# A third set of seven first-layer products in each group of a linear-attention and feed-forward kernel, with all of a group's work in one written order

## The chip, the core and the metric

The kernel runs on one core of a Trainium2 chip. A core has a matrix engine (TensorE, PE in the profile, with its weight loads as PEld), a vector engine (DVE), a scalar engine (ACT), a general engine (POOL) and SyncE (SP), which here issues transfers. Each engine runs its own instructions in program order and waits for others through semaphores. Matrix products go to PSUM, which has eight banks; everything else lies in SBUF. The metric is the time of one execution on the device in microseconds (us).

## What is computed

Retention (linear attention with a decay per head) over q, k and v, and behind it a feed-forward layer on the 4608 resulting tokens:

```python
B, H, S, D_ = q.shape                                  # 8, 8, 576, 64
scores = (1 / np.sqrt(D_)) * np.matmul(q, k.transpose(0, 1, 3, 2))
gamma = 1.0 - 2.0 ** (-5.0 - np.arange(H, dtype=np.float32))
rel = pos[:, None] - pos[None, :]
Dmat = np.where(rel >= 0, gamma[:, None, None] ** rel[None, :, :], 0.0)
attn = np.matmul(scores * Dmat[None, :, :, :], v)
x = attn.transpose(0, 2, 1, 3).reshape(B * S, H * D_)  # 4608 x 512
h = x @ w_in                                           # 512 x 2048
out = np.maximum(0.01 * h, h) @ w_out                  # 2048 x 512
```

## The kernel before

**Units and groups.** The tokens are cut into 36 units of 128 tokens (two chunks of 64; nine chunks make one sequence) and 9 groups of 512 tokens (four units). Group g is put through the feed-forward layer while the units of group g+1 go through retention.

**A unit u** passes these steps. `load` (L121) fetches k, q and v in f32, into a pool of six buffers per kind (`ld_pool`, L70). `cast_k` on ACT, `cast_q` and `cast_v` on POOL (L172 to L181) turn them to f16, with the decay. `transpose_dma` (L183) transposes q and k by a transfer that SP issues. `scores` (L211) makes 64 small products on TensorE's quarters, into the PSUM tile sc (two banks, one buffer): the scores, and the new part of the state. `masks` (L237) applies the causal mask, on DVE; with `aside` an ACT copy is followed by a POOL product. `state` (L257) adds to the running state on DVE, and `state_cast` (L284) makes its f16 copy on POOL. `outputs` (L297) of unit u-1 stands on TensorE right behind the scores of unit u: a first half that needs the masked scores, a second half that needs the f16 states of u-2 and u-1. It fills the PSUM tile ot (two banks, one buffer). `own` (ACT, L370) and `add` (DVE, L376) bring it to xT, the f16 input of the feed-forward layer. `burst` (L791) is these steps from the scores on; `ahead` (L808) is the casts and the transposition of unit u+2; `step` (L823) is both, with the load of unit u+4 between them.

**The first layer** has 16 blocks of 128 features. A plain block (`h_block`, L406) is four products of 128x512 columns into one PSUM bank, and a leaky ReLU on ACT. Four blocks at once (two from each half of the features) can be made by seven half-size products instead of eight, Strassen's scheme in Winograd's form: `h_seven` (L460). It uses sums of w_in (`sum_w_in`, L435, made once) and sums of x (`sum_x`, L447, four POOL operations per group), seven products p1, p1', p6, p5, p7, p5', p7' of four matmuls of 128x256 each, an ACT copy, five DVE additions and four activations. Two sets, at f = 0 and f = 4, make eight of a group's blocks. The other eight (2, 10, 3, 11, 6, 7, 14, 15) are plain. The products take turns in four PSUM banks (`acc_pool`, L80): a new product waits until the bank's contents of four turns ago are read.

**The second layer** is made by the same scheme over 16 blocks (`seven`, L574): seven products P1 to P7' of 16 matmuls of 128x256, with eight sums of the activations per group on DVE (`mix`, L560), some of which overwrite the activations, and sums of w_out made once (`mix_weights`, L545). Each half of a group's result is stored by one transfer of 512 KB on SP (`store`, L516). In the last group the second half is stored in four parts of 128 KB as they come.

**Order of the work.** `manual_schedule` leaves the order to the program text: each engine runs its instructions as they are written. For groups 2 to 8 it comes from nested calls (L949 on): `h_seven` takes plain blocks as fill and a burst in its middle, with some results of a set "owed" to the next one; the mixes and the second layer follow, with steps 7 and 8 in hooks between its products. Group 0 runs plain throughout, in halves as its units arrive; group 1 has a plain first layer, and its second layer is the first use of `seven`; steps 9 to 12 are called in between (`early`, L917, the table `at`, L922, and the hooks at L940). In the opening phase all loads up to unit 10 and the weights are requested on POOL's queue in a fixed order (L673 to L690), and matmuls on zeros (`keep_warm`, L660) fill waits.

```python
def burst(u, out=True, split=False):
    if u < NU:
        scores(u)
    if out:
        outputs(u - 1)
    ...
def early(u, n):
    burst(u)
    ahead(n, (lambda: sum_x(u // 4 - 1)) if u % 4 == 0 else None)
    load(n + 3)
```

## Time and profile before

| | |
|---|---|
| three runs | 283.15, 283.71, 283.88 us (median 283.71) |
| profiled execution | 283.58 us, span of its instructions 281.8 us |
| TensorE matmul busy | 274.0 us (97%), 4231 instructions |
| weight loads | 205.5 us (73%) |
| DVE | 211.7 us (75%) |
| ACT | 153.6 us (55%) |
| POOL | 155.8 us (55%) |
| DMA | 50.04 MB moved, mean 178 GB/s |
| mean granted TensorE clock | 0.997 |

The span runs from the first to the last instruction. Busy time is a union of intervals; matmuls overlap in their pipeline, so the price of a kind of matmul is best read from the distance between starts in the timeline, not from its own duration (a matmul of 128x256 lasts 0.273 us but four of them start 0.44 us after the four before). The same holds for DVE: an addition of 128x512 lasts 0.69 us, and an independent one starts 0.60 us later. In a line of the timeline the columns are start, duration, engine, source line, operation, output and inputs with shape, count, and in brackets the idle time just before it with what ended it.

### The profile page before, as it was taken

The numbers are of one execution on the slowest core, as the hardware profiler recorded it, in microseconds if no ns is written. First come the engines' busy times: TensorE is split into PE (matmuls) and PEld (weight loads), VectorE is DVE, ScalarE is ACT, GpSimd is POOL, SyncE is SP. The second block draws the span as 40 slices with busy tenths as digits, with TensorE's granted clock in tenths as the row PEclk, the third lists the DMA queues.
The fourth block names the chain that finished last, engine by engine and source line by source line (L and its number), as shares of the span: only waits on it lengthen the run. The fifth ranks groups of instructions, "written<-read, shape, count | busy, mean of one in ns | idle before, by whom it ended". The sixth has DMA issues, their size and how long they took to land.

```text
span 281.8 us, 9828 instructions
## 1 busy us (share of the span) xinstructions
PE 274.0 (97%) x4231; PEld 205.5 (73%) x4231; DVE 211.7 (75%) x360; ACT 153.6 (55%) x284; POOL 155.8 (55%) x173
## 2 busy tenths in 40 slices
PE   7899999999999999999999999999999999999994
PEld 3468888745886788678867886788678867886683
DVE  2884688998876887689777986898689677865772
ACT  3776777633337742774277427742774277416610
POOL 8968946735449507960796069607951693051000
PEclk9999999999999999999999999999999999999998
DMA  7999999998999987898689966986797151012004
GB/s 204 309 237 255 280 203 327 211 185 178 230 224 225 270 174 122 230 188 192 149 204 208 215 133 211 223 186 147 198 252 159 40 187 42 2 74 77 0 3 149
DMA packets 123100, 50.04 MB, mean 178 GB/s; under 512 B 112048, under 2 KB 116784, under 8 KB 123056
## 3 DMA queue, kind: packets, MB, share of 16 engines
q1 hardware_dynamic: 116032, 37.23, 59.7%
q0 software_dynamic: 6736, 12.06, 17.7%
q8 instruction: 33, 0.54, 0.8%
q10 hardware_dynamic: 288, 0.11, 0.1%
q14 instruction: 11, 0.09, 0.1%
HBM read 36.81 MB, written 9.44 MB: 164 GB/s over the span
## 4 chain that ended last, share of the span: by engine, by line
PE 87%; DMA 5%; POOL 4%; DVE 3%; issue 1%; ACT 0%; DVEq 0%; POOLq 0%
PE acc L591 35%; PE acc L390 24%; PE acc L471 15%; PE acc L528 5%; POOL t L134 3%; PE sc L221 3%; DMA w_in<-in_moe_w_in_dram 3%; DMA t<-in_v_dram 2%; PE ot L305 2%; PE sc L230 1%; PE ot L316 1%; POOL w_in L152 1%; DVE s L248 0%; DVE xT L377 0%; DVE s L272 0%
## 5 line engine op out<-in xcount | busy, mean ns | idle before, releaser
L390 PE MATMUL acc<-xT,w_in 128*128 128x256 f16 (+2 forms) x496 | 88.6, 318 | 0.1
L591 PEld LDWEIGHTS <-gt 128*128 128x128 f16 x640 | 61.3, 98 | 8.5 <-ACT gt L404 0.8
L404 ACT ACTIVATE gt<-acc 128x512 f16<-128x512 f32 x102 | 58.5, 597 | 13.6 <-PE acc L390 13.1
L390 PEld LDWEIGHTS <-w_in 128*128 128x128 f16 x496 | 45.4, 98 | 18.0 <-issue 0.2
L591 PE MATMUL acc<-w_out,gt 128*128 128x256 f16 x384 | 46.3, 273 | 0.2 <-ACT gt L404 0.2
L372 ACT COPY own<-ot 128x512 f32<-128x512 f32 x33 | 19.4, 587 | 40.3 <-PE ot L316 34.8
L287 POOL CAST st<-s 128x512 f16<-128x512 f32 x21 | 12.9, 612 | 48.3 <-DVE s L272 30.6
L177 POOL TENSOR_TENSOR qk<-t,cs 128x512 f16<-128x512 f32 x28 | 30.5, 1091 | 0.3 <-ACT gt L404 0.2
L591 PE MATMUL acc<-w_mix,gt 128*128 128x256 f16 x256 | 30.6, 273 | 0.0
L181 POOL TENSOR_TENSOR v<-t,cs 128x512 f16<-128x512 f32 x28 | 30.4, 1084 | 0.0
L591 PE MATMUL acc<-w_mix,mix 128*128 128x256 f16 x256 | 29.3, 273 | 0.0
L404 ACT ACTIVATE gt<-h 128x512 f16<-128x512 f32 x42 | 25.7, 629 | 6.0 <-DVE h L482 5.5
L471 PEld LDWEIGHTS <-w_sum 128*128 128x128 f16 x224 | 21.9, 98 | 8.6 <-issue 0.2
L591 PEld LDWEIGHTS <-mix 128*128 128x128 f16 x256 | 25.0, 98 | 3.0
L377 DVE TENSOR_TENSOR xT<-ot,own 128x512 f16<-128x512 f32 x33 | 22.5, 683 | 3.7 <-ACT own L372 3.7
L482 DVE TENSOR_TENSOR h<-acc,u 128x512 f32<-128x512 f32 x28 | 19.2, 686 | 6.0 <-PE acc L471 6.0
L174 ACT CAST qk<-t 128x512 f16<-128x512 f32 x36 | 22.5, 624 | 1.2 <-DMA t<-in_k_dram 1.2
L471 PE MATMUL acc<-x_sum,w_sum 128*128 128x256 f16 x168 | 22.9, 273 | 0.0
L241 POOL TENSOR_TENSOR s<-s,idle 128x512 f16<-128x512 f16 x12 | 13.9, 1160 | 15.8 <-ACT s L240 15.8
L482 DVE TENSOR_TENSOR u<-acc,k 128x512 f32<-128x512 f32 x14 | 9.7, 690 | 17.0 <-PE acc L471 17.0
L471 PEld LDWEIGHTS <-w_in 128*128 128x128 f16 x168 | 16.3, 97 | 6.8 <-DVE h L482 0.5
L489 ACT COPY k<-acc 128x512 f32<-128x512 f32 x14 | 8.2, 586 | 22.2 <-issue 17.0
(77 smaller groups left out, 436.1 us busy)
## 6 DMA issues: line engine op xcount, KB each, us to landing
out_dram<-osb SPq DMA_DIRECT2D x17, 512.0 KB, 4.6
t<-in_k_dram SPq DMA_DIRECT2D x24, 256.0 KB, 4.2
t<-in_q_dram SPq DMA_DIRECT2D x23, 256.0 KB, 4.5
t<-in_v_dram SPq DMA_DIRECT2D x22, 256.0 KB, 4.7
t<-in_v_dram POOLq DMA_DIRECT2D x10, 256.0 KB, 5.4
t<-in_q_dram POOLq DMA_DIRECT2D x9, 256.0 KB, 5.5
t<-in_k_dram POOLq DMA_DIRECT2D x8, 256.0 KB, 5.8
w_in<-in_moe_w_in_dram POOLq DMA_DIRECT2D x8, 256.0 KB, 6.9
```

The source lines that it names most:

```text
L174: nc.scalar.copy(out=qk16[u][:, 1], in_=t32[u, 1])
L177: eng.tensor_tensor(out=qk16[u][:, 0], in0=t32[u, 0], in1=decay(u, 0), op=MUL)
L181: eng.tensor_tensor(out=v16[u], in0=t32[u, 2], in1=decay(u, 1), op=MUL)
L241: nc.gpsimd.tensor_tensor(out=s16s[u], in0=s16s[u], in1=mask16.unsqueeze(1).unsqueeze(1).to_broadcast([P, 2, NP, CH]), op=MUL,)
L372: nc.scalar.copy(out=owns[u], in_=ot_tiles[u][:, :, 0:NP].rearrange("q j c t -> q c j t"))
L377: nc.vector.tensor_tensor(out=x_of(u).rearrange("q (c g) t -> q c g t", g=2), in0=ot_tiles[u][:, :, NP : 2 * NP].rearrange("q g (c j) t -> ...
L390: nc.tensor.matmul(out=hps[:, n, :], lhsT=w_in16[:, c, f * P : (f + 1) * P], rhs=xT[g][:, c, ts], start=(c == 0), stop=(c == NP - 1),)
L404: nc.scalar.activation(out=out, in_=in_, func=mybir.ActivationFunctionType.Lrelu)
L471: nc.tensor.matmul(out=r[name][:, n, :], lhsT=lhs[:, c, n * P : (n + 1) * P], rhs=rhs[:, c, :], start=fresh and n == 0 and c == 0, stop=c ...
L482: nc.vector.tensor_tensor(out=r[name], in0=r[a], in1=r[b], op=ADD)
L528: nc.tensor.matmul(out=ys[tb], lhsT=g_t[0][:, f, tb * P : (tb + 1) * P], rhs=w_out16[:, f, :], start=(f == 0), stop=(f == NF - 1),)
L591: nc.tensor.matmul(out=r[name][tb][:, 0, :] if apart else r[name][0][:, tb, :], lhsT=lhs[:, f, tb * P : (tb + 1) * P], rhs=rhs[:, f, :], s ...
```

## The change

- A third set of seven products at f = 2 replaces the plain blocks 2, 10, 3 and 11. Blocks 6, 7, 14 and 15 stay plain. The sums of w_in get a third tile. The two later sets of these sums are made on POOL instead of DVE, at point 13 of the table `at` and after burst 11.
- The nested calls are replaced by tables of named operations (`set_ops`, `block_ops`, `second_ops`, `step_ops`) and one string, GROUP, that lists all operations of a group in order. The last group has its own string, LAST, and some of its products go to the banks of sc and ot, which no burst uses then (`LAST_HOMES`).
- Partial sums in SBUF are updated in place, in two k, two v and one h buffer. The load pool has five buffers instead of six. A load of unit u+4 is issued behind the transposition of unit u+2.
- In the opening phase v of unit 4 is requested ahead of the third quarter of w_in, two more warming matmuls are added, and the load of unit 13 moves from point 1 to point 4 of the table. In group 1 burst 12 moves from behind P7 to ahead of it.

In the names of the strings, p1A is product p1 of set A (f = 0; B is f = 2, C is f = 4), k, u, v, h4, h5, h4' are its copy and additions, g00 to g11 its activations; blk15 and l15 a plain block and its activation; sc5 the scores of step 5 with the outputs of the unit before; s0, s1a, s1, stc the state and its cast; mc and msk the mask; kc, qc, vc the casts of the unit two ahead; m00 to m31 the mixes; x0 to x3 the sums of x; P1 to P7', K, U, V and o00 to o10 the second layer.

```diff
-    ld_pool = ctx.enter_context(tc.tile_pool(name="ld", bufs=6))
+    ld_pool = ctx.enter_context(tc.tile_pool(name="ld", bufs=5))
...
-    w_sum = const_pool.tile([P, 2, 4, NP // 2, 2 * P], F16, name="w_sum")
+    w_sum = const_pool.tile([P, 3, 4, NP // 2, 2 * P], F16, name="w_sum")
...
-    def masks(u, aside=False):
-        s16s[u] = b_pool.tile([P, 2, NP, CH], F16, name="s16")
-        if aside:
+    def masks_aside(u, part):
+        if part == 0:
+            s16s[u] = b_pool.tile([P, 2, NP, CH], F16, name="s16")
             nc.scalar.copy(out=s16s[u], in_=sc_tiles[u][:, :, 0])
+        else:
             nc.gpsimd.tensor_tensor(
                 out=s16s[u],
                 in0=s16s[u],
                 in1=mask16.unsqueeze(1).unsqueeze(1).to_broadcast([P, 2, NP, CH]),
                 op=MUL,
             )
-            return
+
+    def masks(u):
+        s16s[u] = b_pool.tile([P, 2, NP, CH], F16, name="s16")
...
-    def state(u, j):
+    def state(u, j, parts=(0, 1)):
...
+        if scaled and 0 in parts:
+            nc.vector.tensor_tensor(out=st, in0=st, in1=carry[0], op=ADD)
+        if 1 not in parts:
+            return
...
-    def sum_w_in(f, n):
-        t = w_sum[:, f // 4]
+    def sum_w_in(f, n, eng):
+        t = w_sum[:, f // 2]
...
+    def set_ops(g, f, s, homes):
...
+        ops = {
+            "p1": lambda: product("p1", ws(0, 0), xs(0, 0), True),
+            "k": keep,
+            "p1'": lambda: product("p1", ws(0, 1), xs(1, 0), False),
+            "g00": lambda: give(0, 0, "p1"),
+            "p6": lambda: product("p6", w(1), t(1), True),
+            "u": lambda: into(r["k"], r["p6"], r["k"]),
+            "p5": lambda: product("p5", w(0), t(0), True),
+            "v": lambda: fresh_sum("v", "v", "p5", "k"),
+            "p7": lambda: product("p7", w(2), t(2), True),
+            "h4": lambda: into(r["v"], r["p7"], r["v"]),
+            "p5'": lambda: product("p5", w(3), xs(1, 1), False),
+            "h5": lambda: fresh_sum("h", "h", "p5", "k"),
+            "g11": lambda: give(1, 1, "v"),
+            "p7'": lambda: product("p7", ws(1, 1), t(3), False),
+            "h4'": lambda: into(r["k"], r["p7"], r["k"]),
+            "g01": lambda: give(0, 1, "h"),
+            "g10": lambda: give(1, 0, "k"),
+        }
+        return {n + s: op for n, op in ops.items()}
...
-    def seven(g, last=False):
+    def second_ops(g, homes, last=False):
...
+    def step_ops(g, n):
+        u, w = 4 * g + n, 4 * g + n + 2
+        cast = []
+
+        def mm():
+            if u < NU:
+                scores(u)
+            outputs(u - 1)
+
+        def turn_when_cast(what, *a):
+            what(w, *a)
+            cast.append(0)
+            if len(cast) == 2:
+                transpose_dma(w)
+                if u > 13 and u + 4 < NU:
+                    load(u + 4)
+
+        ops = {
+            "sc": mm,
+            "own": lambda: own(u - 1),
+            "add": lambda: add(u - 1),
+        }
         if u < NU:
-            load(u)
-
-    def step(u, split=False):
-        rest = burst(u, True, split)
-        if u > 13:
-            fetch(u + 4)
-        if u % 4 == 0:
-            sum_x(u // 4 - 1, (0, 1))
-            ahead(u + 2, lambda: sum_x(u // 4 - 1, (2, 3)))
-        else:
-            ahead(u + 2)
-        return rest
+            ops["s0"] = lambda: state(u, 0)
+            ops["s1a"] = lambda: state(u, 1, (0,))
+            ops["s1"] = lambda: state(u, 1, (1,))
+            ops["stc"] = lambda: state_cast(u, pool_copy)
+            if n < 7:
+                ops["mc"] = lambda: masks_aside(u, 0)
+                ops["msk"] = lambda: masks_aside(u, 1)
+            else:
+                ops["msk"] = lambda: masks(u)
+        if w < NU:
+            ops["kc"] = lambda: turn_when_cast(cast_k)
+            ops["qc"] = lambda: turn_when_cast(cast_q, nc.gpsimd)
+            ops["vc"] = lambda: cast_v(w, nc.gpsimd)
+        return {name + str(n): op for name, op in ops.items()}
+
+    SETS = {"A": 0, "B": 2, "C": 4}
+    BLOCKS = (6, 7, 14, 15)
+    GROUP = """
+        p1A kA sc5 p6A qc5 s05 kc5 s1a5 p1'A mc5 p5A uA s15 blk15 own5 vA vc5 g00A add5 p7A
+        msk5 stc5 l15 p1B h4A p5'A h5A kB sc6 kc6 p7'A p1'B p6B mc6 own6 s06 h4'A g00B blk7
+        msk6 s1a6 qc6 p5B uB p1C s16 vB g01A l7 p6C add6 g10A p7B kC h4B g11A p5'B stc6 p1'C
+        g00C sc7 p7'B h5B uC s07 blk14 own7 msk7 p5C blk6 h4'B vC s1a7 p7C g11B p5'C g01B l14
+        vc6 s17 qc7 l6 vc7 h4C stc7 kc7 h5C g11C add7 P1 g01C g10B m00 p7'C sc8 m01 own8 P5
+        h4'C qc8 m10 m11 P6 K g10C m20 vc8 add8 m21 P7 kc8 U s08 V s1a8 m30 P1' x0 x1 m31 P5'
+        s18 o11 x2 stc8 o00 msk8 P7' o01 o10 x3
+    """
+    LAST = """
+        p1A blk6 p6A kA l6 uA p5A vA p7A p1'A p6B g00A p1B p5'A h4A kB h5A p6C p7'A uB p1'B
+        h4'A g00B p5B p7B g10A vB h4B p1C kC blk15 g01A p5'B g11A l15 uC h5B p7'B p5C vC h4'B
+        p1'C g00C p7C blk14 p5'C h4C g11B g01B l14 blk7 g11C l7 h5C m00 p7'C g01C P1 h4'C m01
+        m10 P5 m11 P6 g10C m21 g10B K m20 m31 m30 U V P7 P1' o11 P5' o01 P7' o10 o00
+    """
+    LAST_HOMES = {"B6A": "sc", "B1B": "sc", "B6B": "ot", "B1C": "ot", "Bk7": "ot", "Bk15": "sc", "BP7": "sc"}
...
-    load(4, nc.gpsimd, xs=(1, 0))
+    load(4, nc.gpsimd)
     load_w_in(2)
-    load(4, nc.gpsimd, xs=(2,))
     load(5, nc.gpsimd)
...
     state_last(1)
     first_outputs(1)
+    keep_warm(1)
     state_first(2)
     cast_q(3, nc.vector)
     cast_v(3, nc.vector)
     turn_act(3, 0)
+    keep_warm(1)
...
     def early(u, n):
         burst(u)
-        ahead(n, (lambda: sum_x(u // 4 - 1)) if u % 4 == 0 else None)
+        ahead(n)
         load(n + 3)
 
     at = {
         0: lambda: mixes(1, 0),
-        1: lambda: (ahead(10), load(13)),
+        1: lambda: ahead(10),
         3: lambda: mixes(1, 1),
-        4: lambda: (burst(8, False), ahead(11), load(14)),
+        4: lambda: (burst(8, False), ahead(11), load(13), load(14)),
         7: lambda: mixes(1, 2),
-        12: lambda: [sum_w_in(0, n) for n in range(4)]
+        12: lambda: [sum_w_in(0, n, nc.vector) for n in range(4)]
         + [nc.vector.tensor_copy(out=mask16, in_=mask_sb)],
         9: lambda: early(9, 12),
+        13: lambda: [sum_w_in(2, n, nc.gpsimd) for n in range(4)],
     }
     for n in range(16):
         if n:
@@ -935,40 +1022,35 @@
         if n in at:
             at[n]()
     burst(10)
-    first, others = seven(1)
-    first()
-    others(
-        {
-            0: [lambda: early(11, 13)],
-            2: [lambda: sum_w_in(4, 0), lambda: sum_w_in(4, 1)],
-            3: [lambda: sum_w_in(4, 2), lambda: sum_w_in(4, 3)],
-            4: [lambda: early(12, 14)],
-        }
-    )
+    ops = second_ops(1, {})
+    run = lambda names: [ops[n]() for n in names.split()]
+    run("P1 K m30 m31")
+    early(11, 13)
+    for n in range(4):
+        sum_w_in(4, n, nc.gpsimd)
+    run("P1' o00 P6 U P5 V")
+    burst(12)
+    sum_x(2, (0, 1))
+    ahead(14, lambda: sum_x(2, (2, 3)))
+    load(17)
+    run("P7 o11 P5' o01 P7' o10")
 
     for g in range(2, NG):
-        more = g < NG - 1
-        first, others = seven(g, not more)
-
-        def block(f):
-            return lambda: h_block(g, f)
-
-        def at_step(n, split=False):
-            return (lambda: step(4 * g + n, split)) if more else None
-
-        owed = h_seven(
-            g, 0, [block(2), block(10), block(3), block(11)], at_step(5, True)
-        )
-        owed += [lambda: mix(g, 0, 0), lambda: mix(g, 1, 0)]
-        for late in h_seven(
-            g, 4, [block(6), block(7), block(14), first], at_step(6, True), owed
-        ):
-            late()
-        mix(g, 2, 0)
-        h_block(g, 15)
-        for n in range(3):
-            mix(g, n, 1)
-        others({0: [at_step(7)], 4: [at_step(8)]} if more else {})
+        last = g == NG - 1
+        homes = LAST_HOMES if last else {}
+        ops = second_ops(g, homes, last)
+        for s, f in SETS.items():
+            ops.update(set_ops(g, f, s, homes))
+        for f in BLOCKS:
+            ops.update(block_ops(g, f, homes))
+        if not last:
+            for n in range(5, 9):
+                ops.update(step_ops(g, n))
+            for n in range(4):
+                ops[f"x{n}"] = lambda n=n: sum_x(g + 1, (n,))
+        for name in (LAST if last else GROUP).split():
+            if name in ops:
+                ops[name]()
```

## Prediction

> **What bounds the kernel now.** I read the busy times by stage first. Each row is a stretch, its length, and then busy time and instruction count of PE, PEld, DVE, ACT, POOL, then clock, DMA share and GB/s: one middle group of 512 tokens, and the last group with the tail.
>
> ```profile
> 139.32:167.59 28.27, 28.27 (x458) 21.57 (x457) 22.44 (x38) 16.21 (x30) 16.82 (x19) 1.00 0.92 189
> 252.14:281.80 29.66, 25.71 (x200) 19.03 (x198) 16.28 (x26) 11.23 (x20) 2.59 (x3) 0.97 0.19 72
> ```
>
> TensorE never rests in a middle group. The timeline of TensorE gives its prices by the distance of starts:
>
> ```profile
> 139.15 0.60 PE L471 MATMUL acc<-xT,w_in 128*128 128x256 f16 x4
> 139.59 1.03 PE L390 MATMUL acc<-xT,w_in 128*128 128x512 f16 x4
> 140.47 0.60 PE L471 MATMUL acc<-xT,w_in 128*128 128x256 f16 x4
> ...
> 156.19 1.92 PE L591 MATMUL acc<-w_out,gt 128*128 128x256 f16 x16
> 157.94 3.66 PE L591 MATMUL acc<-w_mix,mix 128*128 128x256 f16 x32
> ```
>
> A product of the first layer takes 0.44, a plain block 0.87, a second-layer product 1.75. A burst (64 small matmuls) takes 0.64 and lengthens the work ahead of it by 0.1. Fourteen products, eight blocks, seven second-layer products and four bursts are 6.1 + 7.0 + 12.25 + 3.0 = 28.3, the measured 28.27: only TensorE work, no wait. So a saving on TensorE counts in full, and so does every wait that the new order puts on it.
>
> **What the change takes from TensorE.** A third set replaces four blocks (4 x 0.87 = 3.46) by seven products (7 x 0.4375 = 3.06): 0.40 less per group. Groups 2 to 7: 6 x 0.40 = **-2.4**.
>
> **What the set adds elsewhere.** Five DVE additions per group. The DVE timeline has such additions back to back at 145.19, 145.78, 146.38: 0.60 each, so 3.0, and 22.4 becomes 25.4 of 27.9. ACT loses four activations and gains four and one copy: 0.5 on 16.2. POOL keeps its work. The tightest place is m00 ahead of P5. In the written order DVE does ahead of it, m00 included, 14 set sums (8.4), six or seven state operations (2.5 to 3.0), three adds and one mask (2.4) and m00 (0.6): 14.2. It starts when burst 5 gives its scores, 1.3 after the group's start, and waits for products on the way, about 1.2 by the same laying out (h4A, vB, h4B): m00 ends at 16.7. On TensorE 21 products, four blocks, four bursts and P1 stand ahead of P5: 9.2 + 3.5 + 3.0 + 1.75 = 17.4. So 0.7 is left, and m01 is needed only for P5's second half. Of the later mixes m21, m30 and m31 fall beside POOL's x0 to x2; a mix beside a POOL operation was seen at 1.03 (148.26) instead of 0.69. I take 0.08 of new waits per group, **+0.5** over six, between 0 and 0.5 each.
>
> **The POOL queue between groups 1 and 2.** Here the change costs. Eight sums of w_in go to POOL: four at point 13 of the table `at`, and four (before on DVE) after burst 11. Their price on POOL isn't in the trace. The nearest row is the sum of x, POOL too, two f16 operands of 128x512: 1.16, four of them 4.6 with their distances (82.73 to 87.31). The lower end is the same w_in sum on DVE, 0.41 alone, the upper end POOL's casts beside busy DVE, 1.49. I take 1.16; at 1.49 the first wait below, and the sum, grow by 1.3. What POOL does there today:
>
> ```profile
> 65.67 1.22 POOL L181 TENSOR_TENSOR v<-t,cs 128x512 f16<-128x512 f32 x1
> 70.31 0.61 POOL L287 CAST st<-s 128x512 f16<-128x512 f32 x1 [3.42 <-DVE s L275]
> 73.59 0.62 POOL L287 CAST st<-s 128x512 f16<-128x512 f32 x1 [2.67 <-DVE s L272]
> ...
> 81.16 0.61 POOL L287 CAST st<-s 128x512 f16<-128x512 f32 x1 [4.94 <-DVE s L275]
> ...
> 88.31 1.16 POOL L241 TENSOR_TENSOR s<-s,idle 128x512 f16<-128x512 f16 x1
> ```
>
> POOL runs strictly in its written order, and its free time here is 3.4 + 2.7 + 4.9 us. All times below are 0.5 earlier than today, for the start-up gain worked out further down.
>
> - First wait. The first four sums start when the casts of unit 12 end, 66.4, and end at 71.0. Behind them stands the state cast of unit 10, ready at 69.8 and now done at 71.6. Burst 11's second output half, which today starts at 71.03 on the heels of that cast (70.31 to 70.92), needs it at 70.5: **+1.1**.
> - Second wait. The state cast of unit 11 starts at 73.4 (73.6 - 0.5, and 0.3 since the mixes ahead of it on DVE run beside the sums). From there POOL has no rest: cast 0.6, q and v of unit 13 2.0, four sums 4.6, cast 0.6, x0 and x1 2.35, q of 14 1.0, x2 and x3 2.2, v of 14 1.0, q and v of unit 15 2.0, and only then the mask product of unit 13, 1.16: in all 17.5, to 90.9. In the new order burst 14 (sc6) stands 7 products, one burst and one block after the group's start: 3.06 + 0.74 + 0.87 = 4.7. The group starts at 82.5 - 0.5 + 1.1 = 83.1, so burst 14 comes at 87.8 and wants the masked scores of unit 13 at 88.1. Today the same burst is at 93.42, 10.9 after the group's start, and the mask product stands ahead of the casts. **+2.8**. The transposed q and k of unit 14 (q cast at about 84.5, 3.7 to land in the DMA view) come at about the same 88.2 and add nothing. Behind burst 14 wait all of TensorE, and DVE and ACT with it. POOL catches up during the stall: later groups have POOL idle before x0.
>
> The trace lets me price a side effect. After the last matmul (278.06) the granted clock is 0.69 between 280.0 and 280.5 and 0.50 after. So 2.2 us of idleness brought the clock down. A second wait of 2.8 could do the same. At the start the warming matmuls at half speed last some 4 us, so about +2.0.
>
> The Trainium skill, "TensorE: Matmul & The Clock Gate", section "What's actually happening", has the clock fall after at least one idle window of 3.4 us, free-running. By that the wait of 2.8 costs no clock and the sum stays. By the trace's 2.2 us it would be 287.2.
>
> **Start-up.** v of unit 4 is now requested ahead of the third quarter of w_in. Today its cast ends a wait that TensorE sees:
>
> ```profile
> 24.98 0.69 DVE L181 TENSOR_TENSOR v<-t,cs 128x512 f16<-128x512 f32 x1 [2.82 <-DMA t<-in_v_dram]
> 25.59 0.75 DVE L209 COPY qkT<-acc 128x512 f16<-128x512 f16 x2
> ```
>
> The copies behind it release burst 4 at 26.39, where TensorE was done at 25.74. The two requests of v swap with those of w_in: 14.8 and 16.4 instead of 17.7 and 19.0, landing 6 later, 22.4. Then the copies follow the transposes (24.64 + 0.3) and end at 25.4: **-0.5**. In exchange w_in's quarter lands at about 25.9 (19.0 + 6.9), and its blocks start at 26.2. If it lands 1 us late the gain turns into +0.3. One load buffer fewer costs nothing: loads 8 to 10 need buffers that were read by 16, 25 and 31.7, and are issued from 32.7 on. The two warming matmuls lie in waits of TensorE of 0.29 and 0.21, a warm one being 0.22; without cover they cost 0.2 each.
>
> **Last group and tail.** Today TensorE starts it at 251.98 and ends P7' at 276.16 + 1.75 = 277.9, 25.9 in all; its work alone is 6.1 + 7.0 + 12.25 = 25.3. Here is the wait:
>
> ```profile
> 266.84 0.60 PE L591 MATMUL acc<-w_out,gt 128*128 128x256 f16 x4
> ...
> 267.66 1.64 PE L591 MATMUL acc<-w_out,gt 128*128 128x256 f16 x12 [0.22 <-ACT gt L404]
> ```
>
> The new order spreads seven of its tiles over the idle sc and ot banks, and puts the last block two places ahead of P1. Laid out like the group above, nothing waits in it (every bank is read out 0.3 or more ahead of its next use, l7 is ready within P1's first half): 21 x 0.4375 + 4 x 0.87 + 12.25 = 24.9, **-1.0**. But o00 is written last, and its store of 512 KB is now SP's last request, behind the two small ones of o10. The end today:
>
> ```profile
> 277.11 0.38 SPq L518 DMA_DIRECT2D out_dram<-osb  x1
> 277.68 1.21 SPq L622 DMA_DIRECT2D out_dram<-osb  x2
> ```
>
> Data moves without a break from 278.0 to 280.05, and the span ends 1.75 later. The large store's data start 0.9 after its issue. Issued at 278.9, it moves from 279.8, and 512 KB at the 400 GB/s of this stretch take 1.3: to 281.1 instead of 280.05, **+1.1** (0.8 to 1.6).
>
> **Sum.** The profiled execution took 283.58 (span 281.8, 1.8 around it), 0.13 under the median 283.71. 283.58 - 0.5 + 1.1 + 2.8 - 2.4 + 0.5 - 1.0 + 1.1 = **285.2**.
>
> **Rivals.**
> - *POOL is in time* (other side): sums of w_in at 0.43, as alone on DVE. The first four end at 68.1, before 69.8: no first wait. The second chain is 2.9 shorter and the group starts 1.1 earlier, so 1.0 of the second wait is left. 285.2 - 1.1 - 1.8 = **282.3**, and 281.3 if that 1.0 is hidden too. It decides from about 0.7 us per sum. For it: f16 runs fast on DVE. Against: POOL's own f16 row.
> - *DVE becomes the bound*: were all eight mixes at 1.03 (today one in a group is), DVE would have 25.4 + 8 x 0.34 = 28.1 of work for 27.9, and with the 1.3 that it waits for each group's first scores TensorE would wait at P5, P6 and P5' for some 0.5 more a group: 285.2 + 3.0 = **288.2**.
> - *The clock falls in the second wait* (priced above): **287.2**. For it the 2.2 us at the end; against it that the wait is only half a microsecond longer, with scores of burst 14 running inside.
>
> **Numbers.** Forecast 0.56 (283.9 to 286.5 by its bounds), POOL in time 0.20, clock 0.12, DVE 0.12. The range 282.1 to 287.8 leaves out some 0.08 of the POOL rival and 0.08 of the DVE rival and the forecast's edges. Within 0.3% of 283.71, about what a measurement can tell, is 282.86 to 284.56: 0.04 from the POOL rival and 0.11 from the forecast, 0.15. Faster 0.16, from the POOL rival alone; slower 0.69.
>
> **What would show it.** Right: in group 2 one gap of TensorE of about 3 ahead of burst 14's second half, ended by POOL's mask product (L246 after); a gap of 1 ahead of burst 11's second half; groups 3 to 7 at 27.9 to 28.0; a sum of w_in on POOL at 1.1 to 1.2; the large store last, the data ending 2.6 after the last DVE addition (278.52 today) instead of 1.5. Wrong: group 2 as long as the others, groups of 28.3 or more, or a clock under 1 in group 2.

## The result, and the profile after

The changed kernel takes **292.11 us** (median of six runs, 291.09 to 293.86) against 283.79 (283.15 to 286.87) before on the same chip: 1.029 times as long, 95% interval 1.023 to 1.035. It is slower, as forecast, but by 8.3 us where 1.5 were forecast (285.2), and outside the range that ended at 287.8. The three runs with a mean clock of 0.999 or 1.000 took 291.1 to 291.7, the three at 0.984 to 0.994 took 292.5 to 293.9. The profiled run is the slowest, 293.86, with a span of 292.1 and a clock of 0.984: 10.3 more than the span of before.

First the stretches, with the columns that the prediction explained (length, busy time and count of PE, PEld, DVE, ACT and POOL, clock, DMA share, GB/s): group 2, one middle group, and the last group with the tail.

```profile
83.86:119.18 35.32, 31.52 (x471) 24.12 (x468) 26.32 (x42) 17.17 (x31) 23.74 (x24) 0.90 0.83 179
119.18:147.76 28.58, 28.11 (x470) 22.59 (x468) 26.53 (x43) 16.89 (x31) 18.32 (x19) 1.00 0.88 186
262.14:292.10 29.96, 25.02 (x214) 20.66 (x211) 19.12 (x31) 11.76 (x21) 0.00 (x0) 0.96 0.19 71
```

TensorE is busy 28.11 of 28.58 us in a middle group, where it was busy without a rest; group 2 takes 35.32, with a mean clock of 0.90. DVE has 26.5 us of work in a group instead of 22.4. From first product to first product of the next group (the last column holds the last group and the tail):

| | start of group 2 | 2 | 3 | 4 | 5 | 6 | 7 | 8 and tail |
|---|---|---|---|---|---|---|---|---|
| before | 82.51 | 28.37 | 28.27 | 28.28 | 28.27 | 28.27 | 28.01 | 29.82 |
| after | 83.86 | 35.32 | 28.58 | 28.97 | 28.56 | 28.88 | 27.97 | 29.96 |

So of the 10.3 us by which the two profiled spans differ, 1.35 came ahead of group 2, 6.95 in group 2, 1.9 in groups 3 to 7, and 0.1 in the end.

**The second wait**, TensorE's timeline in group 2:

```profile
89.15 0.32 PE L225 MATMUL sc<-qkT 64*64 64x64 f16 x16 [0.37 <-DMA qkT<-qk]
...
92.47 0.43 PE L316 MATMUL ot<-s,v 64*64 64x64 f16 x16 [2.79 <-POOL s L246]
...
93.05 1.04 PE L498 MATMUL acc<-x_sum,w_in 128*128 128x256 f16 x4
...
98.71 1.04 PE L498 MATMUL acc<-x_sum,w_sum 128*128 128x256 f16 x8
```

Its releaser is POOL's mask product of unit 13, the last of a chain without a gap since 74.99:

```profile
74.99 0.61 POOL L298 CAST st<-s 128x512 f16<-128x512 f32 x1 [2.67 <-DVE s L284]
...
77.57 1.16 POOL L454 TENSOR_TENSOR w_sum<-w_in 128x512 f16<-128x512 f16 x1
...
91.28 1.14 POOL L246 TENSOR_TENSOR s<-s,idle 128x512 f16<-128x512 f16 x1
```

And behind the wait, five products and a block (3.06 us of work) took 93.05 to 98.71, 5.66. Two rows say why (a stretch, its length, TensorE's busy time, the granted clock): in the 3.41 us up to 91.57 TensorE is busy for 1.16, and then the clock is at half for 6.83 us, though TensorE is at work again from 92.5.

```profile
88.16:91.57 3.41, 1.16 (x38) 1.00 0.89 201
91.57:98.40 6.83, 5.92 (x54) 0.50 1.24 263
```

**In groups 2 to 6** the second half of P5' waits for the last mix (0.43 to 0.47 in the profile). TensorE, DVE and POOL at the end of group 3:

```profile
141.83 2.78 PE L636 MATMUL acc<-w_out,gt 128*128 128x256 f16 x24
145.09 1.05 PE L636 MATMUL acc<-w_out,gt 128*128 128x256 f16 x8 [0.47 <-DVE gt L618]
```

```profile
142.12 2.91 DVE L618 TENSOR_TENSOR gt<-gt,mix 128x1024 f16<-128x1024 f16 x2
```

```profile
140.22 1.47 POOL L469 TENSOR_TENSOR x_sum<-xT 128x512 f16<-128x512 f16 x1 [2.50 <-DVE xT L388]
141.77 1.15 POOL L469 TENSOR_TENSOR x_sum<-xT,x_sum 128x512 f16<-128x512 f16 x1
142.88 1.60 POOL L469 TENSOR_TENSOR x_sum<-xT 128x512 f16<-128x512 f16 x1
```

Two mixes that take 1.28 together alone (0.60 from start to start) take 2.91, each beside POOL's input sums, and those last 1.47 and 1.60 where 1.16 is their length alone.

### The profile page after: what moved, and what is told of

It reads as the page before. It is cut to its first block, busy times and chain, and to the rows that moved or that the text cites. A ratio compares the mean times of both kernels' runs of the same rounds, so it can differ in the third digit from the quotient of the medians.

```text
span 292.1 us, 10069 instructions
## 1 busy us (share of the span) xinstructions
PE 276.1 (95%) x4317; PEld 214.3 (73%) x4317; DVE 240.5 (82%) x391; ACT 158.1 (54%) x291; POOL 170.1 (58%) x181
## 4 chain that ended last, share of the span: by engine, by line
PE 51%; DVE 33%; issue 6%; POOL 5%; ACT 2%; DMA 1%; DVEq 0%; POOLq 0%
PE acc L498 18%; PE acc L401 13%; PE acc L636 9%; DVE gt L618 7%; DVE mix L618 6%; DVE w_mix L599 4%; DVE k L487 3%; DVE xT L388 3%; DVE v L487 3%; PE sc L225 2%; POOL x_sum L469 2%; POOL w_sum L454 2%; DVE w_sum L454 2%; DVE h L487 1%; PE acc L708 1%
## 5 line engine op out<-in xcount | busy, mean ns | idle before, releaser
L401 PE MATMUL acc<-xT,w_in 128*128 128x256 f16 (+2 forms) x376 | 58.6, 300 | 0.3 <-issue 0.3
L415 ACT ACTIVATE gt<-acc 128x512 f16<-128x512 f32 x77 | 45.8, 599 | 19.8 <-PE acc L401 14.6
L498 PEld LDWEIGHTS <-w_sum 128*128 128x128 f16 x336 | 32.9, 99 | 10.7 <-issue 1.1
L487 DVE TENSOR_TENSOR k<-acc,k 128x512 f32<-128x512 f32 x48 | 32.6, 684 | 8.1 <-PE acc L498 6.1
L498 PE MATMUL acc<-x_sum,w_sum 128*128 128x256 f16 x244 | 36.3, 278 | 0.0
L469 POOL TENSOR_TENSOR x_sum<-xT 128x512 f16<-128x512 f16 x14 | 20.8, 1484 | 26.1 <-DVE xT L388 26.1
L185 POOL TENSOR_TENSOR v<-t,cs 128x512 f16<-128x512 f32 x28 | 30.8, 1101 | 0.5 <-DMA t<-in_v_dram 0.5
L521 ACT COPY k<-acc 128x512 f32<-128x512 f32 x19 | 11.1, 586 | 30.7 <-PE acc L498 30.5
L661 ACT COPY osb<-acc 128x512 f32<-128x512 f32 x8 | 4.7, 586 | 37.0 <-PE acc L636 37.0
L498 PE MATMUL acc<-xT,w_in 128*128 128x256 f16 x152 | 23.4, 277 | 0.0
L487 DVE TENSOR_TENSOR v<-acc,k 128x512 f32<-128x512 f32 x29 | 19.9, 686 | 4.1 <-PE acc L498 2.0
```

The costliest lines, as they stand in the source:

```text
L185: eng.tensor_tensor(out=v16[u], in0=t32[u, 2], in1=decay(u, 1), op=MUL)
L401: nc.tensor.matmul(out=hps[:, n, :], lhsT=w_in16[:, c, f * P : (f + 1) * P], rhs=xT[g][:, c, ts], start=(c == 0), stop=(c == NP - 1),)
L415: nc.scalar.activation(out=out, in_=in_, func=mybir.ActivationFunctionType.Lrelu)
L469: nc.gpsimd.tensor_tensor(out=t[:, n], in0=a, in1=b, op=SUB)
L487: nc.vector.tensor_tensor(out=out, in0=a, in1=b, op=ADD)
L498: nc.tensor.matmul(out=r[name][:, n, :], lhsT=lhs()[:, c, n * P : (n + 1) * P], rhs=rhs()[:, c, :], start=fresh and n == 0 and c == 0, sto ...
```

## The experiments

All edits are to the changed kernel, and each is compared with the kernel before on the same chip (medians 283.45 to 283.68). In the expectations *theory A* is that mixes and input sums hold each other up, *theory E*, formed after old_groups and its companions, that it is the passage from the old places of the bursts to the new ones that costs; the rivals are told where they stand. Group distances are read like those of the table above.

### Are the waits in each group made by the input sums?

**no_x_sums** leaves out the four input sums of groups 3 to 8 and uses those of group 2 again, so it computes something else and serves for its times alone.

```diff
+        x_sums[g] = x_sums[2]
-                ops[f"x{n}"] = lambda n=n: sum_x(g + 1, (n,))
+                ops[f"x{n}"] = lambda n=n: None
```

> POOL's four sums of x are left out in groups 2 to 7, so the later groups use old sums; everything else is the changed kernel. Theory A (a mix on DVE, which reads two SBUF operands, cannot run while a POOL operation that reads SBUF runs): the last two mixes m30 and m31 fall from 2.4 to 2.9 us for both to 1.3, the gap of TensorE in the middle of P5' (0.47 in the profile, 0.64 by distance of starts) goes, and groups 3 to 6 fall from 28.56-28.97 to 27.9-28.3 (what is left is m00 and m01 beside a cast). Theory B (DVE simply has too much work between the sets and P5', whoever runs beside it): the mixes keep their length or the gap stays, groups at 28.5 to 28.9.

**mixes_first** keeps all work, and puts the mixes ahead of the input sums (and the mask product of unit 13 ahead of two casts).

```diff
-  ... vc5 g00A add5 p7A msk5 stc5 l15        (qc5 behind p6A)
+  ... g00A add5 p7A msk5 stc5 qc5 vc5 l15
-  m20 vc8 add8 m21 P7 kc8 U s08 V s1a8 m30 P1' x0 x1 m31 P5'
+  m20 vc8 m21 m30 m31 P7 kc8 U s08 V s1a8 add8 P1' x0 x1 P5'
```

> Same work as the changed kernel. m30 and m31 stand right behind m21 on DVE and the add of step 8, which releases the sums of x on POOL, stands behind V; on POOL the mask product and state cast of step 5 stand ahead of the casts of q and v. Theory A: m21, m30 and m31 run alone, 0.6 each, no wait inside P5', groups 3 to 6 at 27.9 to 28.3; the second wait in group 2 falls by the 2.0 us of two casts, and the clock stays at 1 there: in all about 2.0 + 2.6 + 5 x 0.6 under the profiled 293.9, 286 to 287. Theory B: DVE does the same work in another order, so the wait moves to another product and groups stay at 28.5 or more: 288 to 289.

Measured: no_x_sums 291.27 us (one run), mixes_first 289.04 (three runs, 288.31 to 289.78, and a fourth of 293.79; 1.019, 1.016 to 1.023), where theory A had forecast 286 to 287. In both the wait ahead of P5' is gone in all groups. The rows of the mixes that end last (count, then least, median and greatest duration in ns), before, after, and in mixes_first:

```profile
L572 DVE TENSOR_TENSOR gt<-gt,mix x16: 677/685/705, 70.8 to 270.7; 128x1024 f16<-128x1024 f16 x16
```

```profile
L618 DVE TENSOR_TENSOR gt<-gt,mix x16: 678/1347/1639, 72.0 to 279.3; 128x1024 f16<-128x1024 f16 x16
```

```profile
L618 DVE TENSOR_TENSOR gt<-gt,mix x16: 678/680/907, 72.8 to 275.2; 128x1024 f16<-128x1024 f16 x16
```

The median doubled to 1.35 us, and goes back to 0.68 when only the order is changed. So the wait in P5' is made by a mix beside an input sum: theory A is shown for it. In no_x_sums groups 5 and 6 take 27.94 and 28.02, and DVE is busy for 25.0 and 24.5 us in them instead of 26.1 and 26.2: without the input sums the third set's 0.4 comes out nearly whole there (groups 3 and 4 still take 28.99 and 28.34). Groups 3 to 7 of mixes_first take 28.26, 28.25, 28.82, 28.38 and 27.72, 0.3 less in the mean than after, which is about as much as before: most of the 0.4 is still eaten, among others by waits of 0.2 to 0.4 for a mix of P6 in groups 3, 5 and 6, which stands beside POOL's casts. Group 2 takes 30.32 in mixes_first and 32.08 in no_x_sums, so most of what it loses is something else. Both also start it 2.5 later than after (86.33 and 86.47): burst 11 comes 0.9 and 1.0 later, and behind it the clock falls, at 74.2 and 73.9. In mixes_first the wait for the mask product gave way to one of 2.22 for a transposed pair. Neither was in its forecast.

### Is the early loss made by the sums of w_in on POOL, or by the place of the mask product?

**sums_on_dve** makes both later sets of w_in sums on DVE, at the same points.

```diff
-        13: lambda: [sum_w_in(2, n, nc.gpsimd) for n in range(4)],
+        13: lambda: [sum_w_in(2, n, nc.vector) for n in range(4)],
-        sum_w_in(4, n, nc.gpsimd)
+        sum_w_in(4, n, nc.vector)
```

> The two later sets of sums of w_in go from POOL to DVE at the same points of the order; otherwise the changed kernel. If POOL's queue made both waits between groups 1 and 2: burst 11 waits at most 0.5 (after P1 1.96 more than before now), burst 14 in group 2 no longer waits for the mask product (3.3 now), the clock stays at 1 there, and the time falls by about 1.5 + 3.3 + 2.6 from the profiled 293.9, to 286 to 287. Rival: the four sums on DVE ahead of P1' and burst 12 delay DVE's own work, and the waits stay as DVE waits: 290 or more. Groups 3 to 6 stay at 28.6 to 29.0 in both.

**mask_ahead** makes only the first of mixes_first's two edits: mask product and state cast of unit 13 ahead of the casts of unit 15.

> Only change against the changed kernel: on POOL the mask product and state cast of step 5 stand ahead of the casts of q and v of that step. If the second wait is POOL's queue order, it falls from 3.3 us by the two casts, 2.0, to 1.0 to 1.5; too short for the clock to fall, so group 2 takes 31.0 to 31.5 instead of 35.3 (28.6 without any wait). Groups 3 to 6 as in the changed kernel, 28.6 to 29.0; time 289 to 289.5. If the clock's fall came from elsewhere, group 2 keeps some 2.6 more.

Measured: sums_on_dve 292.62 us (1.030, 1.026 to 1.034), mask_ahead 294.47 (1.038, 1.034 to 1.043). Both missed their forecasts (286 to 287, and 289 to 289.5). In both the wait for the mask product falls from 2.79 to 0.54 and 0.68, and neither is faster than after, for another wait is in its place: the transposed q and k of the next units. In sums_on_dve burst 14 waits 1.33 and burst 15 1.91 for them; its mask product itself is hardly earlier (90.95 instead of 91.28). In mask_ahead, a line of TensorE's timeline:

```profile
99.60 0.43 PE L225 MATMUL sc<-qkT 64*64 64x64 f16 x16 [2.69 <-DMA qkT<-qk]
```

Counted from the start of the group, this q is cast 1.3 later and the mask product is made 2.2 earlier. Groups 3 to 6 of mask_ahead take 29.2 to 29.5, some 0.5 more than after, which no run here explains. So the sums alone don't explain group 2; POOL and the transposes are behind the order of the bursts there, whichever comes first on POOL.

### What stays without the third set in the middle groups?

**old_groups** writes the order of before as a string for groups 2 to 6, with two sets and eight blocks, and puts group 1 back (the set at 4 summed on DVE beside P6 and P5). Group 7, last of the middle groups, keeps the changed order. **old_groups_store** is the same with o00 earlier in LAST.

```diff
+        old = g < 7
-        for s, f in SETS.items():
+        for s, f in ({"A": 0, "C": 4} if old else SETS).items():
-        for f in BLOCKS:
+        for f in (2, 10, 3, 11, 6, 7, 14, 15) if old else BLOCKS:
```

```diff
-   ... U V P7 P1' o11 P5' o01 P7' o10 o00
+   ... U V P7 P1' o00 o11 P5' o01 P7' o10     (old_groups_store)
```

> Groups 2 to 6 in the order of before (two sets of seven products, eight plain blocks), group 1 and its w_in sums as before, the third set's four w_in sums on POOL in an idle stretch of group 2; the changed loads, keep-warm matmuls, five load buffers and the changed last group stay. Theory A (the loss sits in group 1, group 2 and in a wait in every group): what stays is start-up -0.8, last group -1.0, tail +1.2 us, so 283.1 us against 283.7 of before, with group distances of 28.3. Rival B (the loss comes with what stays, the five load buffers or the changed loads): 285 us or more, with waits on DMA in groups 1 and 2.

> As old_groups, but in the last group the first half's output copy and its 512 KB store come behind the second product pair (where before has them) instead of at the end. If the tail term is right (the last 512 KB store costs 1.1 to 1.2 us behind the last product): 1.1 us less than old_groups, 282.0 us. If stores of the second half, which are then last, end as late: no difference, 283.1 us.

**third_from_3** has the old order in group 2 alone, and the changed one in groups 3 to 7; **third_casts** has besides all eight mixes ahead of POOL's casts and input sums of that stretch.

> As old_groups_store, with groups 3 to 6 in the changed order with three sets, so that groups 1 and 2 are free of it. Theory A (the wait in each group is made in that group, by POOL's input sums under DVE's mixes): groups 3 to 6 keep the 28.6 to 29.0 us that they have in the changed kernel, and the whole is 282.0 + 1.9 = 283.9 us. Rival C (the waits in groups 3 to 6 are an aftermath of the late group 2): 27.9 us each, 282.0 - 1.6 = 280.4 us.

> As third_from_3, but in groups 3 to 6 all eight mixes of a group come ahead of POOL's two casts and four input sums of that stretch. Theory A (a mix of two SBUF operands is held by a POOL operation that reads SBUF beside it): the waits ahead of P6, P5 and P5' go, 27.9 to 28.1 us a group, 282.0 - 1.0 = 281.0 us. Rival D (POOL, DVE and the transposes have no room left, so that the wait only moves to a transposed pair or an input sum that is now late): 28.4 us or more, 282.6 us or more.

Measured: 292.06 (1.029, 1.024 to 1.033), 289.97 (1.024, 1.020 to 1.028), 292.32 (1.030, 1.027 to 1.034) and 293.44 us (1.034, 1.031 to 1.038): all four expectations missed. The group distances show why.

| | start | 2 | 3 | 4 | 5 | 6 | 7 | 8 and tail |
|---|---|---|---|---|---|---|---|---|
| old_groups | 83.20 | 30.82 | 28.39 | 28.26 | 28.40 | 28.28 | **33.19** | 29.96 |
| old_groups_store | 81.88 | 30.81 | 28.40 | 28.26 | 28.41 | 28.28 | **33.30** | 28.76 |
| third_from_3 | 82.27 | 30.82 | **34.10** | 28.83 | 28.57 | 29.00 | 28.05 | 28.76 |
| third_casts | 83.48 | 30.82 | **35.26** | 29.68 | 28.02 | 28.96 | 27.77 | 28.71 |

Whichever group is the first in the changed order, 7 or 3, takes 33 to 35 us, though group 1 is as before and the sums of w_in lie far ahead (in third_from_3 the last one on POOL ends 9 us ahead of group 3, with 3.9 of rest behind it). In third_from_3's group 3 TensorE waits twice, and the clock falls behind the second wait:

```profile
115.86 0.60 PE L498 MATMUL acc<-x_sum,w_sum 128*128 128x256 f16 x4 [1.53 <-POOL x_sum L469]
...
122.20 0.36 PE L316 MATMUL ot<-s,v 64*64 64x64 f16 x16 [2.32 <-POOL s L246]
```

```profile
122.00:123.00 1.00, 0.80 (x34) 0.67 (x34) 0.00 (x0) 0.04 (x1) 1.00 (x3) 0.67 1.06 391
123.00:124.00 1.00, 1.00 (x6) 0.74 (x5) 0.13 (x1) 0.55 (x1) 1.00 (x2) 0.50 1.38 249
```

That gave theory E. The changed order asks for a group's first burst 0.5 after its start and for the second 4.7 after; before it was 3.6 and 10.9. The group ahead has made its input sums and casts at the old pace. (Group 2's 30.8 comes with these kernels' own edit, the set at 2 summed on POOL beside mixes; in two_sets, without it, it is 28.3.) The store is settled by two rows of this table and not by the medians: the last group and tail shrink by 1.2 when o00 comes early. In third_casts the wait ahead of P5' became one for V of up to 1.1, DVE being late: the rival of that expectation.

### Two sets with what is left of the change, and the third set at the old places

**two_sets** takes the old order for all of groups 2 to 7, makes the sums of the set at 2 on DVE behind the state work of unit 4, and keeps the changed start-up and the last group with o00 early. **old_places** adds the third set in the middle groups, with bursts, casts, mixes and input sums in the old places.

```diff
     settle(4)
+    for n in range(4):
+        sum_w_in(2, n, nc.vector)
...
-        p1A kA blk2 l2 p1'A g00A blk10 l10 p6A uA p5A vA sc5 ... blk3 l3 p7A h4A p5'A h5A ...   (two_sets)
+        p1A kA p1B kB p6A uA p1'A g00A p5A vA p1'B g00B sc5 ... p7A h4A p6B uB p5'A h5A ...     (old_places)
```

> Groups 2 to 7 in the order of before, two sets and eight plain blocks each, group 1 and its sums as before; only the last group has three sets, and its four w_in sums are made on DVE where the trace shows it idle, behind the state work of unit 4. Changed start-up and changed last group stay; the first half's last output copy and its store are put back ahead of the second half's. Theory E (what costs 5 to 7 us is the passage from the old order to the new one: bursts 1 and 2 of a group come some 3 and 5 us earlier in it, and POOL has the masked scores ready only at the old place): no such passage ahead of the last group, group distances 28.3, so 283.5 - 0.75 (start-up) - 1.0 (last group) = 281.8 us. Rival B (the five load buffers, the changed loads or the last group cost): 284 us or more.

> As two_sets, but groups 2 to 7 have the third set of products, in another written order: the bursts, the casts, the mixes and the input sums stand where the order of before has them, and the third set takes the places of the four plain blocks. Theory E (place of the bursts) and theory A (input sums under mixes) both say that the waits go: group distances of 27.9 to 28.0, 281.8 - 2.1 = 279.7 us. Rival D (DVE has 25.4 us of work in a group of 27.9 and is late somewhere): distances of 28.3 or more, 281.8 us or more, with waits on DVE.

Measured: two_sets **282.26 us** (281.73 to 282.71, twelve runs): 0.995 of before, 0.994 to 0.997, faster than both kernels. Group 2 starts at 82.00, groups 2 to 7 take 28.0 to 28.4, the last group with the tail 28.76 instead of 29.82. So nothing that stays costs anything (rival B falls), though the gain is small, 1.2 us in the medians. old_places takes 295.33 us (1.042, 1.038 to 1.045), 30.0 to 30.8 a group. Its group 4:

```profile
145.13 0.60 PE L498 MATMUL acc<-x_sum,w_sum 128*128 128x256 f16 x4 [0.63 <-POOL x_sum L469]
...
150.19 0.61 PE L498 MATMUL acc<-x_sum,w_in 128*128 128x256 f16 x4 [0.66 <-DVE v L487]
```

With two sets side by side and no plain blocks between them, seven products take TensorE 3.06 us and their five additions take DVE 3.0: DVE works almost without a break from 148.2 to 155.1 and TensorE waits for it. That is the rival of that expectation. It isn't DVE alone: p6 of the first set, now earlier in the group, waits for POOL's input sum as well, 0.63 in the line above and 0.2 to 1.6 in each of the groups 2 to 7.

### No sum on POOL at all, and a softened passage

**sums_early** is the changed kernel with the set at 2 summed as in two_sets, the set at 4 and the load of unit 13 as before, o00 early, and GROUP as it is. **late_second** has besides mixes_first's order, and in group 2 alone the second and third burst about 3 us later.

> The changed kernel with its order of groups 2 to 7 as it is, but no w_in sum on POOL: the third set's four are made on DVE in an idle stretch behind the state work of unit 4, those of the set at 4 on DVE beside P6 and P5 of group 1 as before; the store of the last group's first half is early again. The account of the prediction (eight POOL sums make the first wait and the wait for unit 13's mask product): both waits go, group 2 takes 28.7 as groups 3 to 6, and the whole is 282.3 (two_sets) + 6 x 0.4 = 284.7 us. Theory E (POOL and the transposes are late in any group that follows the old phase, with or without the sums): the first wait goes, but group 2 still takes 32 us or more, 288 us or more.

> As sums_early, with the mixes ahead of the input sums in groups 2 to 7 (as in mixes_first), and in group 2 alone the second burst some 3.5 us and the third some 3 us later among the products, near their old places. Theory E: group 2 takes 28.0 to 29.0, the others 28.3 as in mixes_first, and the whole is 282.3 (two_sets) + 0.5 = 282.8 us. Rival F (group 3 then meets the same passage, one group later): one group of 31 us or more, 286 us or more.

Measured: sums_early 289.47 us (1.021, 1.018 to 1.024), clock 1.000, group 2 31.35; late_second 286.99 (1.013, 1.009 to 1.016), group 2 31.14 and the others 27.7 to 28.9. For sums_early, TensorE in group 2, and POOL:

```profile
90.55 0.32 PE L316 MATMUL ot<-s,v 64*64 64x64 f16 x16 [1.00 <-POOL s L246]
...
96.66 0.32 PE L225 MATMUL sc<-qkT 64*64 64x64 f16 x16 [0.76 <-DMA qkT<-qk]
```

```profile
80.21 0.61 POOL L298 CAST st<-s 128x512 f16<-128x512 f32 x1 [4.36 <-DVE s L286]
...
89.34 1.16 POOL L246 TENSOR_TENSOR s<-s,idle 128x512 f16<-128x512 f16 x1
```

Without any sum POOL rests 4.4 us, for burst 12, and then needs 9.1 us of casts and input sums to the mask product: 1.0 late, with 0.19, 0.51 and 0.76 for transposed pairs. So of group 2's 35.3 the sums make 4.0, about what 1.8 of the mask's wait and the clock's fall come to, and the 2.65 above the 28.7 of after's groups 3 to 6 are the passage. (Groups 3 and 4 of sums_early are longer too, 29.53 and 29.02.) Both accounts were half right. The first wait, which both had expected to go, only changed its cause: bursts 11 and 12 now wait 0.75 and 0.81 for transposed pairs, and group 2 starts at 83.51, where after has 83.86 and two_sets 82.00. In late_second group 2's waits for POOL and for transposed pairs are gone, and nothing is handed on to group 3 (28.26; rival F falls), but group 2 loses the same, once 0.53 to ACT and the rest mostly to DVE, whose sums are now bunched with the mixes; the 282.8 of its expectation was missed by 4:

```profile
102.39 0.32 PE L316 MATMUL ot<-s,v 64*64 64x64 f16 x16 [0.55 <-DVE xT L388]
...
103.43 3.97 PE L636 MATMUL acc<-w_mix,mix 128*128 128x256 f16 x32 [0.58 <-DVE mix L618]
```

Not tried: an order that spreads the passage over several groups, and one with three sets in which no mix meets a POOL operation at all.

## Why the prediction was right or wrong, by its own steps

**Start-up, -0.5: right.** Burst 4 starts at 25.68 instead of 26.39 (-0.7). Its copies follow the transposes, v's cast having lost its wait:

```profile
22.05 0.69 DVE L185 TENSOR_TENSOR v<-t,cs 128x512 f16<-128x512 f32 x1
23.82 0.42 DVE L213 COPY qkT<-acc 128x512 f16<-128x512 f16 x1 [1.08 <-PE acc L206]
```

**First wait, +1.1: the burst right, the engine and the size wrong.** P1 to P1' of group 1 took 4.81 instead of 2.85, +1.96. The price of a sum was right (1.15 to 1.33 in place of 1.16), and POOL's state cast was late as laid out (71.72), but the wait came sooner, at the scores, from DVE:

```profile
71.59 0.32 PE L225 MATMUL sc<-qkT 64*64 64x64 f16 x16 [1.92 <-DVE s L286]
```

```profile
67.16 1.37 DVE L454 TENSOR_TENSOR w_sum<-w_in,w_sum 128x512 f16<-128x512 f16 x1
68.45 1.14 DVE L1015 CAST idle<-cs 128x64 f16<-128x64 f32 x1
```

The same instructions before, with the two sums ahead of them, which stood beside POOL's casts (64.49 to 66.89):

```profile
64.84 1.15 DVE L443 TENSOR_TENSOR w_sum<-w_sum,w_in 128x512 f16<-128x512 f16 x1
65.91 1.26 DVE L443 TENSOR_TENSOR w_sum<-w_in 128x512 f16<-128x512 f16 x1
67.09 0.41 DVE L443 TENSOR_TENSOR w_sum<-w_in,w_sum 128x512 f16<-128x512 f16 x1
67.43 0.18 DVE L929 CAST idle<-cs 128x64 f16<-128x64 f32 x1
```

The last of DVE's own sums of w_in (1.37 where it was 0.41) and the small cast behind it (1.14 where it was 0.18) ran beside POOL's. The step counted what POOL's sums queue on POOL, and not what they hold up on DVE.

**Second wait, +2.8: right as a wait.** 0.5 ahead of burst 14 and 2.8 within it, for POOL's mask product, as laid out. POOL's chain took 17.4 (74.99 to 92.42) where 17.5 were added up. That the wait within the burst is 2.8 to the digit is partly luck: the mask product ended 1.5 later than laid out (92.4 against 90.9), and the burst came 1.4 later too (89.15 against 87.8). The rival in which POOL is in time left "1.0 of the second wait"; sums_early, which takes the sums away altogether, shows 1.00, in another kernel than the rival's.

**The clock: the rival came true beside the forecast.** It was priced at 2.0 and given 0.12; in the profiled run it cost 5.66 - 3.06 = 2.6. The granted clock fell 1.9 us after the scores that stand inside the wait (89.7 to 91.57): they did not protect it, as the rival's counterargument had it. The Trainium skill, "TensorE: Matmul & The Clock Gate", section "What's actually happening", has the clock fall after an idle window of some 3.4 us that runs freely. The length of the window agrees with the trace (last section), but it need not be idle: 1.16 us of work in it were too little. The trace's own 2.2 us at the end of before was the better guide, though it was the end of a window and not a length of rest: the 3.41 us up to that fall (276.77 to 280.18) hold 1.30 of work. Three of the six runs show a clock under 0.995. The clock alone didn't put the time outside the range: the three runs at 0.999 or 1.000 took 291.1 to 291.7.

**New waits per group, +0.08: this is the step that failed.** "I take 0.08 of new waits per group, +0.5 over six, between 0 and 0.5 each." Against the 27.87 that the saving leaves, groups 3 to 6 took 0.7 to 1.1 more. The step named the place (m21, m30 and m31 beside POOL's x0 to x2) and priced it by the one mix of before that was seen beside a POOL operation, 1.03. The median is 1.35, up to 1.64, since the input sums follow each other without a gap, and P5' had no room for it. The trace of before had nearer rows: DVE's sums of w_in, 0.41 alone, took 1.15 and 1.26 beside POOL's casts (the lines above). Over groups 3 to 7 a gain of 1.6 became a loss of 1.9. The Trainium skill, "SBUF — State Buffer", section "Who interferes with whom", says that a DVE instruction with two SBUF inputs contends with a POOL instruction that reads SBUF, and calls the ports that they share an exclusive lock. The rows agree: 0.68 alone, 1.35 in the median beside the sums. By that rule, as an estimate, a mix beside x0 to x3 takes its own 0.68 and at most one 1.16 of POOL, up to 1.84; the greatest measured, 1.64, lies within that and above 1.03.

**The passage: missing, a term put at nothing.** Group 2 lost 6.95 where +2.8, -0.4 and 0.1 were written. 0.5 of the rest is the second wait's size, 2.6 the clock, and the remaining 1.4 smaller losses in the group (0.47 of them at P5'). The prediction had asked what delays the mask product, but not what else an order that wants a group's first two bursts 3 and 6 us earlier asks of POOL and SP: sums_early shows 1.5 for transposed pairs in group 2, where it said that they "add nothing" at burst 14.

**The third set, -2.4: right for TensorE's work, and seen in single groups only.** (4 x 0.87 is 3.48 and not 3.46, which changes nothing.) A dense group would take 27.9: groups 5 and 6 of no_x_sums take 27.94 and 28.02, group 5 of third_casts 28.02, and group 7 of mixes_first, which has few casts, 27.72 against 28.01 before. In after the saving is eaten by DVE, with 26.5 us in a group where 25.4 were forecast, held up by POOL.

**Last group -1.0 and tail +1.1: right.** Together +0.14 in the trace of after. The large store is last on SP:

```profile
282.24 5.74 SPq L666 DMA_DIRECT2D out_dram<-osb  x4
288.07 0.38 SPq L564 DMA_DIRECT2D out_dram<-osb  x1
```

and in two_sets it stands ahead of the two small ones, which brings the 1.06 of the last group out:

```profile
275.70 0.38 SPq L564 DMA_DIRECT2D out_dram<-osb  x1
276.27 1.21 SPq L666 DMA_DIRECT2D out_dram<-osb  x2
```

In sum, of the 8.7 us between the predicted +1.6 and the measured +10.3 in span, 3.5 are the groups' waits, 4.45 group 2 (2.6 of it the clock) and 0.75 the first wait.

## What to carry to other kernels

Where two engines hold each other up, price each operation beside the other engine's whole train of operations, not by one sighting; then see whether the wait has room at that place. A new order of a pipelined loop is paid twice: in its steady state, and in the first round, when the stages ahead still run at the old places; look at that round by itself. A saving on the busiest engine is worth trying first where the others have slack: the last group kept its 1.0 us, the middle ones none.

## What the runs showed of the hardware that was not expected

- A small cast on DVE (128x64) took 1.14 us beside POOL's sum of two SBUF operands, and 0.18 alone. It ended at 69.59, when the POOL sum that had started ahead of it (68.32) ended, at 69.54, so nearly all of its time looks like waiting for it.
- The clock goes by windows, not by the length of a rest. Half speed lasted 6.83 us in after and 3.41 us in no_x_sums and third_from_3: two times and one time 3.41. Full speed too comes in whole numbers of this step: in the traces' records of the clock it lasted 85.33 us ahead of the fall in after (25 steps) and 273.07 us in before (80 steps). Read back from the falls in such steps, the window ahead of a fall held 1.16 us of TensorE work in after, 1.49 in no_x_sums, 1.09 in third_from_3. In after's first wait, a rest of 1.9 us as long as that of no_x_sums at the same place, a step ends at 71.10, inside the rest; the window up to it holds 1.99 us of work, and the clock stayed. First after, then no_x_sums:

```profile
67.69:71.10 3.41, 1.99 (x32) 1.00 0.86 195
```

```profile
70.46:73.87 3.41, 1.49 (x70) 1.00 1.03 232
73.87:77.29 3.42, 3.42 (x19) 0.50 1.36 274
```

That the windows run on without regard to the rest is inferred from these lengths. It would explain why one kernel shows the fall in some runs only. In mixes_first a window with 1.68 us of work (70.78 to 74.19) brought the clock down, and in old_places one with 1.79 (81.60 to 85.01) did not. So in these traces the limit lies between the two, about half of a window; no run was made to find it.
